# Expert selection in front of the one-hot table, an earlier pump, and w1's first remainders on VectorE

## The chip, the cores and the metric

The kernel runs on one core of one Trainium2 chip. The engines are TensorE (PE in the profile; its weight loads are PEld), VectorE (DVE), ScalarE (ACT), GpSimd (POOL) and SyncE (SP), and 16 DMA engines. The metric is the device time of one execution in microseconds (us).

## The reference

Three stages follow one another: windowed attention, a mixture of experts with one expert per token, and a dense feed-forward layer with a squared ReLU.

```python
# q, k, v: (4, 8, 576, 64); heads 0-3: 32 keys back; heads 4-7: 128 keys back, every 4th
scores = np.where(masks, q @ k.T / 8, -1e9)
x = softmax(scores) @ v              # -> (2304, 512)
logits = x @ w_gate + modality_bias[modality_id]
e_idx = np.argmax(logits, axis=1)    # one of 8 experts per token
for e in range(8):
    mask = e_idx == e
    h = np.maximum(x[mask] @ w1[e], 0.0)        # w1: (512, 1024) per expert
    out[mask] = gate_w[mask, None] * (h @ w2[e])  # w2: (1024, 512) per expert
h = np.maximum(out @ w_in, 0.0)      # w_in: (512, 2048)
result = h * h @ w_out
```

With the inputs of this case all tokens go to two experts.

## The kernel before, in words

Attention is cut into 48 units: 4 batches, two kinds of mask, 6 tiles of 96 queries. `schedule` runs rounds i = 0, 1, 2, ...; one round does the scores of unit i (`A`, lines 323 and 326), the transposes of x for the gate of unit i - 5 (`H`, L401), the transposes of the probabilities of unit i - 2 (`D`, L348), the product with v of unit i - 3 (`F`, L362, with the three VectorE instructions L365, L368 and L371) and, at the end of each group of six, the gate's logits. Every engine executes its instructions in the order in which this loop issues them.

Between these pieces `schedule` lets two other streams advance. `filler` runs matmuls of the experts' slots: it is called twice a round with FILL / 2 each, and each step of the stream costs an amount that is drawn from it. `step` runs the routing of a finished batch: `route` turns the logits of 576 tokens into positions (small VectorE instructions, L442 to L514), builds one-hots (L520, L521; on GpSimd, for batch 2 on VectorE), waits LATE[b] rounds, and multiplies the one-hots on TensorE (L527) into the table `tbl` of token numbers by expert column (L528 to L532). `select` (from L534) then chooses for two or four slots of 128 tokens which expert and which column of the table they take, some twenty VectorE instructions on one partition, and ends by casting the table to `itab` (L634).

When a batch's `side` stream is over, `schedule` calls `moe.pump`. It begins up to three slots (`begin`: SP and GpSimd load numbers from `esel`; GpSimd copies a column of itab to sc, L706, and gathers 128 rows of x from DRAM, L707, 128x513 words, 262 KB) and then stages weights (`stage`, L677: SP issues the DMAs of 2 MB each for w1 and w2 of slot 0). SP also stores x (L375, L379), and loads q, k and v (L298, L306, L294); GpSimd also scales q (L304).

A slot's work is: transposes of the gathered rows (`tx`, L714), xh on ScalarE and xl on VectorE; splitting w1 into a rounded part (ScalarE, L686) and a remainder (L687); the first layer (L728); transposes of its result (`th`, L741) with hth on ScalarE and htl on VectorE (L744); the second layer (L758). Slot 0 waits six empty filler calls between the pump and its transposes. Both weights are split for slot 0; later slots split only where the expert changes. In the function `split`, the first two remainders of w1 of slot 0 go to GpSimd, all others to VectorE.

After the attention the remaining slots run together with the decoding of w_in and w_out, and then the feed-forward layer, which is the longest part.

Of the kernel before, what the change touches and what calls it, by code (L numbers as in the profile page):

```python
# [11 lines left out]
F32 = mybir.dt.float32  # L12
F32R = mybir.dt.float32r
BF16 = mybir.dt.bfloat16
F16 = mybir.dt.float16
# [3 lines left out]
ALU = mybir.AluOpType  # L19
# [9 lines left out]
QT, KT = 96, 128  # L29
# [5 lines left out]
NCOL = E * NTT  # L35
TPB = S // QT
# [2 lines left out]
NA = 6  # L39
UPB = 2 * TPB  # L40
WAVES = ((0, 2), (2, 4), (NA, NSLOT - NA))
RATE, RATE1, RATE2, FILL, BURST, GAP = 0.35, 0.5, 0.5, 3.0, 0.0, 3
SETUP = 3
START = (("q", 0, 3), ("m", 0, 0), ("i", 0, 0), ("v", 0, 3), ("q", 3, 6), ("v", 3, 6))
LATE = (5, 5, 2, 7)
TINY = float(np.array([0x38100000], np.int32).view(np.float32)[0])


# [16 lines left out]
def body(ctx, tc, ins, out):  # L65
# [15 lines left out]
    with ExitStack() as mctx:  # L81
        moe = Moe(g, mctx)
        with ExitStack() as actx:
            att = Attention(g, actx)
            att.warm(9)
            with tc.manual_schedule():
                schedule(att, moe)
        ffn = Ffn(g, ctx)
        with tc.manual_schedule():
            for cost in moe.slots(NA, NTT):  # L90
                if not cost:
                    ffn.side()
            ffn.rest()
            moe.extras()
            moe.tag()
            ffn.l1(0, 0)
            ffn.l1(0, 1)
            run(moe.l2(NSLOT - 1))
        mctx.close()
        ffn.run()  # L100
# [6 lines left out]
def run(steps):  # L107
    for _ in steps:
        pass


def schedule(att, moe):
    nu = B * UPB
    moe.banks((2, 4), (4, 2), (2, 2), (7, 7))
    side, fc, sc, hold, nxt, due = None, 0.0, 0.0, 0, 0, 0
    i = 0
    fill, more = moe.slots(0, NA), True

    def step(cost):
        nonlocal side, sc, hold  # L120
        if i < hold:
            return
        sc += cost
        while side is not None and sc > 0 and i >= hold:
            c = next(side, None)
            if c is None:
                side = None
            elif c == 0:
                hold, sc = i + 1, 0.0
            else:  # L130
                sc -= c
        sc = min(sc, 0.0)

    def one():
        step(0.01 - sc)

    def filler(cost, late):
        nonlocal more, fc
        fc += cost
        while more and fc > 0:  # L140
            c = next(fill, None)
            if c is None:
                more = False
            elif c == -2 and late:
                fc = max(fc, BURST)
            elif c < 0:
                fc = 0.0
            else:
                fc -= c
        fc = min(fc, 0.0)  # L150

    for i in itertools.count():
        att.tail = i >= nu + 2
        ns, no, nh = (2, (5,), (5,)) if att.tail else (2, (5,), (6,)) if moe.ready else (3, (5, 4), (7,))
        r = RATE2 if i >= nu + 5 else RATE1 if moe.prepped else RATE
        if i == nu + 2:
            moe.banks((2, 4), (6, 0), (1, 1), (7, 3))
        att.A(i, (0, 1, 2)[:ns])
        if i == SETUP:
            att.setup()  # L160
        if NTL < i <= nu + 5 and i % NTL == 5:
            att.logits(i // NTL - 1, 1)
            if moe.ready and not att.tail:
                no, nh = nh, no
        if i > hold:
            step(r)
        att.H(i - 5, nh)
        filler(FILL / 2, False)
        att.D(i - 2)
        step(r)  # L170
        att.F(i - 3, no, one)
        att.C(i)
        filler(FILL / 2, True)
        step(r)
        if NTL < i <= nu + 5 and i % NTL == 4:
            att.logits(i // NTL - 1, 0)
        if due and side is None:
            moe.ready = sum(WAVES[due - 1])
            moe.pump()
            due = 0  # L180
        if nxt < B and side is None and i >= (nxt + 1) * UPB + 5:
            side = itertools.chain(att.route(nxt), att.select(*WAVES[nxt - 1]) if nxt else ())
            due, sc, hold = nxt, 0.0, i + 1
            nxt += 1
        if not more:
            break
    run(side or ())
    if due:
        moe.ready = NSLOT
        moe.pump()  # L190


class Attention:
# [236 lines left out]
    def route(self, b):  # L430
        nc, rt, iota = self.g.nc, self.rt, self.g.iota

        def new(shape, name, dt=F32):
            return rt.tile(shape, dt, tag=name, name=name)
# [3 lines left out]
        for i in range(TPB):  # L438
# [17 lines left out]
                                       op0=ALU.is_equal, op1=ALU.mult)  # L456
# [53 lines left out]
        cf, rf = new([QT, TPB], "rcf"), new([QT, TPB], "rrf")  # L510
# [1 line left out]
        nc.vector.tensor_copy(cf, ci)  # L512
        yield 0.12
        nc.vector.tensor_copy(rf, ri)  # L514
        rhot, val = new([QT, TPB, 128], "rhot", F16), new([QT, TPB, NCOL], "rval", F16)
        eng = nc.vector if b == 2 else nc.gpsimd
        for i in range(TPB):
            if b == 2:
                yield 0.5
            eng.tensor_scalar(out=rhot[:, i, :], in0=iota[:QT, :128], scalar1=rf[:, i:i + 1], scalar2=None, op0=ALU.is_equal)  # L520
            eng.tensor_scalar(out=val[:, i, :], in0=iota[:QT, :], scalar1=cf[:, i:i + 1],  # L521
                              scalar2=self.tok[:, i:i + 1], op0=ALU.is_equal, op1=ALU.mult)
        for _ in range(LATE[b]):
            yield 0
        psi = self.bank()[:, :NCOL]
# [1 line left out]
            nc.tensor.matmul(psi, rhot[:, i, :], val[:, i, :], start=i == 0, stop=i == TPB - 1)  # L527
        nc.vector.tensor_tensor(out=self.tbl, in0=psi, in1=self.tbl, op=ALU.add)  # L528
        if b:
            off = new([128, NCOL], "roff")  # L530
            nc.vector.tensor_scalar(out=off, in0=psi, scalar1=float(b * S), scalar2=float(b * S), op0=ALU.mult, op1=ALU.min)
            nc.vector.tensor_tensor(out=self.tbl, in0=self.tbl, in1=off, op=ALU.add)  # L532

    def select(self, j0, n):  # L534
        nc, rt, g = self.g.nc, self.rt, self.g
        last = j0 + n == NSLOT
        k = f"{j0}"

        def new(shape, name, dt=F32):
            return rt.tile(shape, dt, tag=name, name=name)  # L540
# [21 lines left out]
                                in1=cum.unsqueeze(1).to_broadcast([1, n, E]), op=ALU.is_ge)  # L562
# [27 lines left out]
        w = new([1, NSLOT, E], "sw")[:, :n, :]  # L590
# [38 lines left out]
            yield 0.12  # L629
            nc.vector.tensor_tensor(out=self.taken, in0=self.taken, in1=tk, op=ALU.add)  # L630

        it = g.moe.itab[{0: 0, 2: 1, 6: 2}[j0]]
        yield 0.12
        nc.vector.tensor_scalar(out=it, in0=self.tbl, scalar1=-1.0, scalar2=0.0, op0=ALU.add, op1=ALU.max)  # L634
        for j in range(j0, j0 + n):
            g.moe.itab_of[j] = it


class Moe:
    def __init__(self, g, ctx):  # L640
# [38 lines left out]
    def split(self, j, w):  # L679
        nc, tc = self.g.nc, self.g.tc  # L680
        c = self.chg[j][2]
        src, hi, lo = self.st[w], self.wh[w], self.wl[w]
        n = src.shape[1]

        def part(k, eng=nc.vector):
            nc.scalar.activation(out=hi[:, k, :], in_=src[:, k, :], func=AF.Copy)  # L686
            eng.tensor_tensor(out=lo[:, k, :], in0=src[:, k, :], in1=hi[:, k, :].bitcast(F32), op=ALU.subtract)  # L687

        if j == 0:
            for k in range(n):  # L690
                part(k, nc.gpsimd if w == 0 and k < 2 else nc.vector)
                yield -1
            return
        with tc.If(c > 0, preferred_fallthrough_block=False):
            for k in range(n):
                part(k)

    def begin(self, j):
        nc, g = self.g.nc, self.g
        e = nc.values_load(g.esel[0:1, 0, j:j + 1], engines=(ET.SP,), min_val=0, max_val=E - 1)  # L700
        c = nc.values_load(g.esel[0:1, 1, j:j + 1], engines=(ET.SP,), min_val=0, max_val=1)
        split = nc.values_load(g.esel[0:1, 1, j:j + 1], engines=(ET.Activation, ET.DVE), min_val=0, max_val=1)
        col = nc.values_load(g.esel[0:1, 2, j:j + 1], engines=(ET.Pool,), min_val=0, max_val=NCOL - 1)
        self.chg[j] = (e, c, split)
        sc = self.sc[j % 3]
        nc.gpsimd.tensor_copy(sc, self.itab_of[j][:, bass.ds(col, 1)])  # L706
        nc.gpsimd.indirect_dma_start(out=self.gx[j % 3], out_offset=None, in_=g.xd[0:2 * S if j < 2 else 3 * S if j < 6 else NT, :],  # L707
                                     in_offset=bass.IndirectOffsetOnAxis(ap=sc.bitcast(U32), axis=0))
# [375 lines left out]
```

## Time and profile before

| | us |
|---|---|
| median of 3 runs | 816.04 |
| lowest and highest | 813.96, 816.46 |
| the profiled execution | 815.87 |
| its span | 814.1 |
| TensorE busy | 784.6 (96%) |
| VectorE busy | 418.9 (51%) |
| ScalarE busy | 325.1 (40%) |
| GpSimd busy | 173.9 (21%) |

The mean granted TensorE clock was 0.99 of full speed. Times of the profile count from the start of the span. A row of a timeline has the start, the time to the end of the group, the engine, the line, the operation, output and inputs, and in square brackets how long the engine had been idle before it and what ended that; "x4" means four instructions in one row. "Busy" of a matmul group overlaps its neighbours a little, so the distance of two starts is the better measure of what a group takes. In a table of windows each row is a stretch with its length, then the busy time and the number of instructions of PE, PEld, DVE, ACT and POOL in this order, the granted clock (1.00 is full speed), the DMA engines' busy share and GB/s.

### The profile page before, as it was taken

The numbers are of one execution on the slowest core, as the hardware profiler recorded it, in microseconds if no ns is written. First come the engines' busy times: TensorE is split into PE (matmuls) and PEld (weight loads), VectorE is DVE, ScalarE is ACT, GpSimd is POOL, SyncE is SP. The second block draws the span as 40 slices with busy tenths as digits, with TensorE's granted clock in tenths as the row PEclk, the third lists the DMA queues.
The fourth block names the chain that finished last, engine by engine and source line by source line (L and its number), as shares of the span: only waits on it lengthen the run. The fifth ranks groups of instructions, "written<-read, shape, count | busy, mean of one in ns | idle before, by whom it ended". The sixth has DMA issues, their size and how long they took to land.

```text
span 814.1 us, 12599 instructions
## 1 busy us (share of the span) xinstructions
PE 784.6 (96%) x4273; PEld 671.7 (83%) x4273; DVE 418.9 (51%) x1124; ACT 325.1 (40%) x779; POOL 173.9 (21%) x234
## 2 busy tenths in 40 slices
PE   8999987899999999998989899999999999999996
PEld 5888866788888888887877799989989989998995
DVE  5787888444257777441799942242242233224222
ACT  5777766232245554541444522232232222223221
POOL 4254731231123333110255610010000001001001
PEclk9999998999999999999999999999999999999999
DMA  7766681201234443722245410010001001001001
GB/s 225 188 177 163 177 279 43 68 27 46 72 118 119 140 130 100 247 91 72 80 115 147 127 39 26 1 52 27 1 13 39 27 14 39 1 0 39 1 1 39
DMA packets 44810, 67.40 MB, mean 83 GB/s; under 512 B 6816, under 2 KB 28672, under 8 KB 44224
## 3 DMA queue, kind: packets, MB, share of 16 engines
q1 hardware_dynamic: 38720, 50.75, 21.6%
q0 software_dynamic: 3280, 10.76, 4.3%
q10 hardware_dynamic: 2736, 4.99, 1.6%
q8 instruction: 35, 0.57, 0.3%
q14 instruction: 39, 0.32, 0.1%
HBM read 129.65 MB, written 14.44 MB: 177 GB/s over the span
## 4 chain that ended last, share of the span: by engine, by line
issue 40%; DVE 5%; PE 2%; DMA 2%; POOL 1%; ACT 1%; POOLq 0%; ACTq 0%; DVEq 0%; SPq 0%
DMA raw<-in_wo 2%; POOL out L995 1%; DVE da L880 1%; PE bk L945 1%; DVE fhl L964 1%; DVE da L874 1%; DVE da L869 1%; PE bk L758 1%; DVE da L877 1%; PE bk L990 1%; ACT dm L867 0%; ACT woh L884 0%; DVE fsq L955 0%; DVE yl L932 0%; DVE fout L994 0%
## 5 line engine op out<-in xcount | busy, mean ns | idle before, releaser
L955 DVE TENSOR_TENSOR fsq<-fr 128x384 f32<-128x384 f32 x84 | 46.9, 559 | 173.3 <-ACT fr L953 173.3
L945 PE MATMUL bk<-yh,wih 128*128 128x384 f32 x384 | 130.7, 340 | 3.2 <-ACTq L827 1.6
L945 PE MATMUL bk<-yl,wih 128*128 128x384 f32 x384 | 130.3, 339 | 1.3 <-DVE yl L932 1.3
L945 PE MATMUL bk<-yh,wil 128*128 128x384 f32 x384 | 129.9, 338 | 0.0
L953 ACT ACTIVATE fr<-bk 128x384 f32<-128x384 f32 x96 | 46.9, 488 | 187.9 <-PE bk L945 187.3
L990 PE MATMUL bk<-woh,fhh 128*128 128x512 f32 x288 | 114.6, 398 | 2.7 <-ACT woh L884 2.7
L990 PE MATMUL bk<-wol,fhh 128*128 128x512 f32 x288 | 113.4, 394 | 2.9 <-POOL wol L885 2.9
L990 PE MATMUL bk<-woh,fhl 128*128 128x512 f32 x288 | 113.3, 393 | 0.0
L995 POOL DMA_INDIRECT out<-fout,fidx x18 | 18.1, 1006 | 323.3 <-DVE fout L994 320.5
L945 PEld LDWEIGHTS bk<-yh,wih 128*128 128x128 f32 x384 | 72.6, 189 | 8.3 <-ACT yh L931 2.2
L964 DVE TENSOR_TENSOR fhl<-fsq,fhh 128x384 fp32r<-128x384 f32 x96 | 55.4, 578 | 45.0 <-ACT fhh L963 44.7
L945 PEld LDWEIGHTS bk<-yl,wih 128*128 128x128 f32 x384 | 72.7, 189 | 5.8 <-DVE yl L932 2.6
L945 PEld LDWEIGHTS bk<-yh,wil 128*128 128x128 f32 x384 | 72.7, 189 | 0.0
L963 ACT ACTIVATE fhh<-fsq 128x384 fp32r<-128x384 f32 x96 | 50.4, 525 | 50.2 <-DVE fsq L955 48.7
L990 PEld LDWEIGHTS bk<-wol,fhh 128*128 128x128 f32 x288 | 54.1, 188 | 14.2 <-POOL wol L885 5.9
L728 PE MATMUL bk<-w1h,xh 128*128 128x512 f32 x152 | 64.1, 421 | 0.8 <-DVE htl L744 0.8
L990 PEld LDWEIGHTS bk<-woh,fhl 128*128 128x128 f32 x288 | 54.0, 188 | 12.9 <-DVE fhl L964 0.4
L990 PEld LDWEIGHTS bk<-woh,fhh 128*128 128x128 f32 x288 | 54.1, 188 | 12.2 <-ACT woh L884 4.2
L728 PE MATMUL bk<-w1l,xh 128*128 128x512 f32 x152 | 61.6, 405 | 0.0
L728 PE MATMUL bk<-w1h,xl 128*128 128x512 f32 x152 | 61.5, 404 | 0.0
L758 PE MATMUL bk<-w2h,hth 128*128 128x512 f32 x152 | 61.0, 401 | 0.0
L758 PE MATMUL bk<-w2h,htl 128*128 128x512 f32 x152 | 59.5, 391 | 0.0
(173 smaller groups left out, 1375.9 us busy)
## 6 DMA issues: line engine op xcount, KB each, us to landing
st<-in_w SPq DMA_DIRECT2D x41, 2048.0 KB
raw<-in_wi SPq DMA_DIRECT2D x32, 256.0 KB
raw<-in_wo SPq DMA_DIRECT2D x32, 256.0 KB
v<-in_v SPq DMA_DIRECT2D x7, 780.0 KB
q<-in_q SPq DMA_DIRECT2D x7, 576.0 KB
kd<-in_k SPq DMA_DIRECT2D x14, 288.0 KB
xd<-x SPq DMA_DIRECT2D x40, 96.0 KB
yb<-y ACTq DMA_DIRECT2D x13, 256.5 KB
```

Source lines behind the costliest of these rows:

```text
L728: nc.tensor.matmul(ps, a[:, c, :], w[:, c, sl], start=k == 0, stop=k == 11)
L758: nc.tensor.matmul(ps, a[:, c, :], w[:, c, :], start=k == 0, stop=k == 23)
L869: nc.vector.tensor_scalar(out=a, in0=raws[new][:, :, 1], scalar1=3, scalar2=0x3FFFFFF8, op0=ALU.logical_shift_left, op1=ALU.bitwise_and)
L874: nc.vector.scalar_tensor_tensor(out=a, in0=raws.pop(old)[:, :, 0], scalar=29, in1=a, op0=ALU.logical_shift_right, op1=ALU.bitwise_or)
L877: nc.vector.scalar_tensor_tensor(out=a, in0=raws[new][:, :, 1], scalar=-0x40000000, in1=a, op0=ALU.bitwise_and, op1=ALU.bitwise_or)
L945: nc.tensor.matmul(ps, w[:, c, f * 128:(f + 1) * 128], a[:, c, :], start=k == 0, stop=k == 11)
L953: nc.scalar.activation(out=r, in_=ps, func=AF.Relu)
L955: (nc.gpsimd if blk == 0 and f > 3 else nc.vector).tensor_tensor(out=s, in0=r, in1=r, op=ALU.mult)
L963: nc.scalar.activation(out=hh, in_=s, func=AF.Copy)
L964: nc.vector.tensor_tensor(out=hl, in0=s, in1=hh.bitcast(F32), op=ALU.subtract)
L990: nc.tensor.matmul(acc[t], a[:, sl], w[:, f, :], start=f == 0 and j == 0, stop=f == NF - 1 and j == 2)
L995: dma = nc.gpsimd.indirect_dma_start(out=out, out_offset=bass.IndirectOffsetOnAxis(ap=self.idx[:, i:i + 1].bitcast(U32), axis=0), in_=o, i ...
```

## The change

The one-hots move into a function `onehots`, the table into `table`, and a new generator `batch` runs `route`, then `select`, then `table`. Before, the order was route with the table, then select. For batches 0, 1 and 3 the one-hots are still issued at the end of `route`, on GpSimd; for batch 2 they are issued in `table`, on VectorE. `itab` is now made at the end of `table`. The rounds between the one-hots and their matmuls, LATE, go from 5, 5, 2, 7 to 5, 2, 1, 4. FILL goes from 3.0 to 2.0. In `split` the first two remainders of w1 go to VectorE with the others.

```diff
-RATE, RATE1, RATE2, FILL, BURST, GAP = 0.35, 0.5, 0.5, 3.0, 0.0, 3
+RATE, RATE1, RATE2, FILL, BURST, GAP = 0.35, 0.5, 0.5, 2.0, 0.0, 3
-LATE = (5, 5, 2, 7)
+LATE = (5, 2, 1, 4)
@@ schedule
-            side = itertools.chain(att.route(nxt), att.select(*WAVES[nxt - 1]) if nxt else ())
+            side = att.batch(nxt)
@@ route
-        rhot, val = new([QT, TPB, 128], "rhot", F16), new([QT, TPB, NCOL], "rval", F16)
+        self.hots = cf, rf, new([QT, TPB, 128], "rhot", F16), new([QT, TPB, NCOL], "rval", F16)
+        if b != 2:
+            yield from self.onehots(b)
+
+    def onehots(self, b):
+        nc, iota = self.g.nc, self.g.iota
+        cf, rf, rhot, val = self.hots
         eng = nc.vector if b == 2 else nc.gpsimd
         for i in range(TPB):
-            if b == 2:
-                yield 0.5
+            yield 0.5 if b == 2 else 0.01
             eng.tensor_scalar(out=rhot[:, i, :], ...)
             eng.tensor_scalar(out=val[:, i, :], ...)
+
+    def table(self, b):
+        nc, rt = self.g.nc, self.rt
+        rhot, val = self.hots[2:]
+        if b == 2:
+            yield from self.onehots(b)
         for _ in range(LATE[b]):
             yield 0
         psi = self.bank()[:, :NCOL]
...
             nc.vector.tensor_tensor(out=self.tbl, in0=self.tbl, in1=off, op=ALU.add)
+            yield 0.12
+            it = self.g.moe.itab[b - 1]
+            nc.vector.tensor_scalar(out=it, in0=self.tbl, scalar1=-1.0, scalar2=0.0, op0=ALU.add, op1=ALU.max)
+
+    def batch(self, b):
+        moe = self.g.moe
+        yield from self.route(b)
+        if b:
+            j0, n = WAVES[b - 1]
+            yield from self.select(j0, n)
+            for j in range(j0, j0 + n):
+                moe.itab_of[j] = moe.itab[b - 1]
+        yield from self.table(b)
@@ select
-        it = g.moe.itab[{0: 0, 2: 1, 6: 2}[j0]]
-        yield 0.12
-        nc.vector.tensor_scalar(out=it, in0=self.tbl, scalar1=-1.0, scalar2=0.0, op0=ALU.add, op1=ALU.max)
-        for j in range(j0, j0 + n):
-            g.moe.itab_of[j] = it
@@ split
-        def part(k, eng=nc.vector):
+        def part(k):
             nc.scalar.activation(out=hi[:, k, :], in_=src[:, k, :], func=AF.Copy)
-            eng.tensor_tensor(out=lo[:, k, :], in0=src[:, k, :], in1=hi[:, k, :].bitcast(F32), op=ALU.subtract)
+            nc.vector.tensor_tensor(out=lo[:, k, :], in0=src[:, k, :], in1=hi[:, k, :].bitcast(F32), op=ALU.subtract)
         if j == 0:
             for k in range(n):
-                part(k, nc.gpsimd if w == 0 and k < 2 else nc.vector)
+                part(k)
                 yield -1
```

The lines of the kernel after are some 18 higher in the experts' part: L714 becomes L732, L728 becomes L746, L707 becomes L725 and L677 becomes L695; the table's matmuls L527 become L538.

SP's queue around the first weights (st_81 is w1, st_82 is w2, xd<-x a store of x, esel the numbers of the chosen experts), in the kernel before:

```order
L379 DMA xd<-x 96x256
L379 DMA xd<-x 48x256 x2
L379 DMA xd<-x 96x256
L294 DMA v<-in_v 128x1560
L375 DMA xd<-x 96x256 x2
L700 TENSOR_LOAD esel
...
L677 DMA st_81<-in_w 128x4096
...
L677 DMA st_82<-in_w 128x4096
```

and in the kernel after:

```order
L379 DMA xd<-x 48x256 x2
L718 TENSOR_LOAD esel
...
L695 DMA st_81<-in_w 128x4096
...
L695 DMA st_82<-in_w 128x4096
L379 DMA xd<-x 96x256
L294 DMA v<-in_v 128x1560
L375 DMA xd<-x 96x256 x4
```

The weights have moved ahead of one load of v and three stores of x.

GpSimd's queue around the first gather, in the kernel after (q scaling, the load of the column number, the copy of the column, the gather):

```order
L526 TENSOR_SCALAR rval<-iota,rcf,tok 96x144
L304 TENSOR_SCALAR q<-q 128x192 [waits DMAHW0_49,PE_49,Pool_49]
L304 TENSOR_SCALAR q<-q 128x192 x5
L721 TENSOR_LOAD esel [waits DVE_49]
...
L724 COPY sc_97<-itab_104 128x1 [waits DVE_49]
L725 DMA gx_90<-xd,sc_97 128x513 [waits DMAHW5_49,DMAHW6_49,DMAHW3_49,DMAHW7_49,DMAHW2_49,Pool_49]
```

Here nothing has moved: before, too, the first gather stands right behind the same six scalings of q.

TensorE's queue in round 41 (L422 are the logits, L401 the transposes of x, L348 those of the probabilities), in the kernel before:

```order
L326 MATMUL bk_67<-kd_139,q 96x256 x2
...
L401 MATMUL bk_71<-ident,x 128x96 x2
L348 MATMUL bk_69<-ident,p 128x96 x4
L362 MATMUL bk_72<-v,pt 96x65 x4
L323 LDWEIGHTS mask
```

and in the kernel after:

```order
L422 MATMUL bk_72<-xtl,wg 16x288
L401 MATMUL bk_71<-ident,x 128x96 x2
L732 MATMUL bk_68<-ident,gx_90 128x128 x4
L348 MATMUL bk_69<-ident,p 128x96 x4
L362 MATMUL bk_72<-v,pt 96x65 x4
```

Slot 0's transposes now stand in round 41; before they stand at the same place of round 44.

## Rows read from the trace of the kernel before

**Rows 1.** Busy time of each engine, whole span (page, first part).
```profile
PE 784.6 (96%) x4273; PEld 671.7 (83%) x4273; DVE 418.9 (51%) x1124; ACT 325.1 (40%) x779; POOL 173.9 (21%) x234
```

**Rows 2.** Windows: stretch, length, PE, PEld, DVE, ACT, POOL busy, clock, DMA, GB/s.
```profile
94.58:96.81 2.23, 2.23 (x21) 1.94 (x21) 1.70 (x5) 1.83 (x7) 2.23 (x4) 1.00 0.62 96
106.90:146.45 39.55, 31.93 (x223) 25.57 (x222) 33.62 (x105) 25.62 (x67) 7.02 (x5) 0.91 0.42 144
110.90:121.70 10.80, 9.43 (x80) 8.07 (x81) 9.47 (x44) 8.13 (x24) 1.36 (x1) 1.00 0.94 364
126.20:133.00 6.80, 6.20 (x21) 4.85 (x22) 6.73 (x17) 2.68 (x7) 0.00 (x0) 0.50 0.07 19
146.60:150.10 3.50, 3.50 (x9) 2.73 (x10) 2.59 (x22) 0.00 (x0) 0.18 (x1) 0.51 0.05 15
```

**Rows 3.** Timeline of TensorE, 96 to 152 us.
```profile
97.89 0.33 PE L401 MATMUL bk<-ident,x 96*128 96x96 f32 x2
98.06 0.49 PE L348 MATMUL bk<-ident,p 96*128 96x96 f32 x4
98.39 0.54 PE L527 MATMUL bk<-rval,rhot 96*128 96x144 f16 x6
98.77 0.84 PE L362 MATMUL bk<-v,pt 128*96 128x65 f32 x8
...
107.53 0.33 PE L401 MATMUL bk<-ident,x 96*128 96x96 f32 x2
...
116.68 0.60 PE L714 MATMUL bk<-ident,gx 128*128 128x128 f32 x4
...
126.81 1.54 PE L362 MATMUL bk<-v,pt 128*96 128x65 f32 x8 [3.04 <-DVE x L371]
...
146.49 0.68 PE L728 MATMUL bk<-w1h,xh 128*128 128x512 f32 x1 [0.76 <-DVE htl L744]
```

**Rows 4.** Timeline of GpSimd, 99 to 130 us.
```profile
99.66 4.01 POOL L304 TENSOR_SCALAR q<-q 128x192 f32<-128x192 f32 x6 [2.74 <-PE bk L362]
...
107.44 1.18 POOL L707 DMA_INDIRECT gx<-xd,sc  x1 [0.85 <-DMA v<-in_v]
...
109.10 0.98 POOL L707 DMA_INDIRECT gx<-xd,sc  x1 [0.27 <-POOL sc L706]
120.34 4.67 POOL L687 TENSOR_TENSOR w1l<-st,w1h 128x1024 fp32r<-128x1024 f32 x2 [10.27 <-ACT w1h L686]
```

**Rows 5.** Timeline of VectorE, 99 to 144 us.
```profile
99.75 0.30 DVE L544 TENSOR_SCALAR sci<-carry 1x8 int32<-1x8 f32 x1
...
105.65 0.21 DVE L634 TENSOR_SCALAR itab<-tbl 128x144 int32<-128x144 f32 x1
...
120.93 1.80 DVE L514 CAST rrf<-rri 96x6 f32<-96x6 int32 x1
...
122.92 2.18 DVE L520 TENSOR_SCALAR rhot<-iota,rrf 96x128 f16<-96x128 f32 x1
...
125.36 0.27 DVE L520 TENSOR_SCALAR rhot<-iota,rrf 96x128 f16<-96x128 f32 x1
...
126.68 1.21 DVE L687 TENSOR_TENSOR w1l<-st,w1h 128x1024 fp32r<-128x1024 f32 x1
...
143.32 0.15 DVE L544 TENSOR_SCALAR sci<-carry 1x8 int32<-1x8 f32 x1
```

**Rows 6.** Timeline of SP's DMA issues, 98 to 99 and 106 to 110 us.
```profile
97.86 0.78 SPq L379 DMA_DIRECT2D xd<-x  x2
...
106.43 0.30 SPq L375 DMA_DIRECT2D xd<-x  x1
109.58 0.38 SPq L677 DMA_DIRECT2D st<-in_w  x1
```

**Rows 7.** Gathers by tile gx, 104 to 120 us: two gathers.
```profile
DMA to landing us min/median/max: 3.5/6.2/8.8
```

**Rows 8.** Gathers by tile gx, 320 to 336 us: two gathers.
```profile
DMA to landing us min/median/max: 3.8/6.9/10.0
```

More of the change, by code (lines that the diff above doesn't have):

```diff
@@ L529, in route @@
         if b:
-            off = new([128, NCOL], "roff")
+            off = rt.tile([128, NCOL], F32, tag="roff", name="roff")
             nc.vector.tensor_scalar(out=off, in0=psi, scalar1=float(b * S), scalar2=float(b * S), op0=ALU.mult, op1=ALU.min)
             nc.vector.tensor_tensor(out=self.tbl, in0=self.tbl, in1=off, op=ALU.add)
+            yield 0.12
[10 more added lines that the diff above has]
+        yield from self.table(b)
     def select(self, j0, n):
```

## The prediction

> **What bounds the kernel now.** I read the page first: TensorE (PE) is busy 784.6 of 814.1 us [rows 1]. So an edit pays only where PE waits, and I looked at PE's idle time by windows. Outside the decode of wi and wo, which the change does not touch, PE waits in one stretch: 106.9 to 146.45, between the selection for batch 1 and the start of slot 1's first matmuls. There PE is busy 31.93 of 39.55 us, the mean granted clock is 0.91, and VectorE (DVE) is busy 33.62 [rows 2]. VectorE has more to do there than in a plain round of attention, where it is busy 1.70 of 2.23 us [rows 2]: the splits of both weights, xl, htl, the routing of batch 2 and its one-hots. PE follows it.
>
> The timeline of PE gives the marks [rows 3]: in round 41 it starts the x transposes (L401) at 107.53; slot 0's transposes (L714) stand three rounds later, at 116.68; the longest wait, 3.04 us, ends at 126.81; and slot 1's first matmul starts at 146.49, when htl's second half is in. This last one is my milestone: behind it VectorE has slack and PE stays nearly full in both kernels, so a gain or loss there goes straight to the end. Around the 3.04 us of waiting the granted clock fell to 0.50, the lower of the two levels, and stayed there from 126.2 to 133.0; it cost little, since VectorE was busy 6.73 of these 6.80 us [rows 2]. It was 0.51 again from 146.6 to 150.1, behind the milestone, where PE was busy all the time [rows 2]: half of 3.5 us, 1.7, is lost there.
>
> What made the 3.04 us is in VectorE's and GpSimd's (POOL's) timelines side by side. GpSimd ran the first two remainders of w1, 4.67 us from 120.34 [rows 4]. In that time a small cast at VectorE's L514 took 1.80, and the one-hot L520 took 2.18, against 0.27 for the same L520 at 125.36 [rows 5]. With 0.16 for the small cast (the price of the small copies beside it, an estimate) the two lost 3.55 us.
>
> **The change, part by part.**
>
> *Remainders on VectorE.* Two of 1.21 [rows 5] are added, 2.42 less an overlap with the neighbours of 0.15, 2.27; 3.55 go. Net gain 1.3 on the engine that bounds the stretch. GpSimd's 4.67 fall away where nothing waited for it.
>
> *Selection ahead of the table, table two rounds after the one-hots.* Batch 1's selection moves from rounds 38 to 40 to rounds 33 to 35, where VectorE has 0.5 us a round free [rows 2], beside GpSimd's one-hots. The only rows with selection beside GpSimd are those at 99.75: L544 0.30 against 0.15 at 143.32 [rows 5], while GpSimd scaled q [rows 4]. Twenty operations at +0.15 are 3.0 us over three rounds, against 1.6 free; so up to 1.4 late, down to nothing if most overlap. But rounds 38 to 40 get the room back that the selection took there until 105.65 [rows 5]. I take zero, with 0.6 either way. The Trainium skill, "SBUF — State Buffer", section "SBUF: two separate sides", says that GpSimd and a VectorE instruction with two SBUF inputs share a port pair as an exclusive lock, the other blocks for the whole instruction. By that rule the 2.18 is the wait for one remainder of 2.36, and the trace agrees there; the selection beside q scaling it overstates, for no row there waits out a whole scaling of 0.68.
>
> *The pump three rounds earlier.* Selection and itab end in round 37, so SP issues the weights and GpSimd the gathers about 7 us sooner, and slot 0's transposes stand in round 41, right behind the L401 that began at 107.53. The two issuers don't move alike, and this is the term that decides.
>
> SP: in the order after, the esel loads follow the two half x stores of round 37, which SP issued by 98.64 [rows 6]. From the last x store's end (106.73) to the first weight DMA (109.58) the loads took 2.85; so the weights are issued at about 101.5 and 102.1 and, as before (when 121.7 was the end, 12.1 us behind the issue; 364 GB/s on the mean from 110.9 on [rows 2]), are in by about 113.6. The v load that stood ahead of them now stands behind both; it lands about 115.5, and round 45 needs it, later than that: no cost.
>
> POOL: the six q scalings still stand ahead of the first esel load. They started at 99.66, when q had come, and ended at 103.67 [rows 4]; q's load and the rounds around it don't move. Before, 1.6 us passed from itab's end (105.65 + 0.21) to the gather at 107.44 [rows 4, 5], with the load of the column number partly ahead of it; I take 2, an estimate, so gather 0 is issued at about 105.7, four microseconds behind the weights. Before, gather 0 was issued at 107.44, ahead of them, and landed in 3.5; gather 1, issued at 109.10 with the weights right behind it, took 8.8 [rows 4, 7]. In a later slot a gather beside weights took 10.0, the other 3.8 [rows 8]. A gather behind the weights thus lands with their end. I take 8.8: 114.5; bounds 109.2 (3.5) and 115.7 (10.0).
>
> PE reaches slot 0's transposes at about 107.2 (a little sooner than 107.53, since rounds 38 to 40 carry no selection), executes in order, and waits until 114.5: 7.3 us idle, VectorE soon too. Queued behind are the whole of round 41's rest and all that follows.
>
> *The sum to the milestone.* VectorE's own work before, 106.9 to 146.45: 33.62 − 3.55 = 30.1. After, to the same htl: + 2.27; + 16 selection operations of batch 2, which now precede it, at 0.15 less overlaps, 1.9; − the table's three, 0.8, − one pair of one-hots, 0.5, − two attention tails (x and two small ones), 1.1, − one remainder of the transposed x, 0.3: 31.7, an estimate. Some 1.8 of it, about what a round has, lies ahead of the wait. After the landing: 0.6 for four transposes and 0.65 for xh, so xl starts at 115.75; 29.9 of VectorE work; gaps, of which the stretch had 5.9 before, 3 to 4: the milestone at about 149.1. Up to there PE has done less than before: two groups each of L401, L348, L362 and the six table matmuls. By the starts from 97.89 to 98.77 and L362's 0.84, less some 0.18 by which it overlaps what follows [rows 3], that is 2 × (0.17 + 0.33 + 0.66) + 0.38 = 2.7. So 149.1 + 2.7 = 151.8 stands against 146.49 + 1.7 = 148.2: +3.6.
>
> *Slot 2's transposes.* They stand some 4 us of PE work behind batch 2's table matmuls, before 13. Table to itab is four operations, 1.2; itab to gather issue was 1.8 (105.65 to 107.44) and the landing 3.5 [rows 4, 5, 7]: 6.5 against 4 to 5.5. I take +1, from 0 to 2.5.
>
> *Batch 3's table, the smaller FILL.* One slot sooner, its gather beside no weights; PE work is the same and VectorE has slack: nothing, unless a copy waits (0.3). The smaller share moves matmuls of the slots into later rounds and beyond the attention, where they fill PE as well; its part at the milestone is in the counts above.
>
> Sum: the profiled execution took 815.87 with a span of 814.1, 0.17 under the median. +3.6 + 1 gives 820.5; I say 820, since work that piles up in the wait may fill VectorE's gaps better. If the clock falls again behind the milestone, 1.7 is to be added: 822. That is some 4 above the median; a difference under 0.3%, 2.45 us, I call none.
>
> **Rivals.**
>
> *A. The gather is hardly delayed; VectorE's gaps stay.* Landing at 109.5 to 111, PE waits 2 to 4. xl starts at 110.8 to 112.3, the milestone is 144 to 146, and the total 816 ± 1.5. For it: a gather is 262 KB, the weights 4.2 MB. Against it: the two rows of 8.8 and 10.0. The Trainium skill, "DMA: Bandwidth & Descriptors", section "Queues, rings and completion order", says that each DMA engine takes turns between queues packet by packet. That would double some 0.7 us of transfer (262 KB at 364 GB/s, an estimate) and speaks for A; the 8.8 and 10.0 are against it.
>
> *B. Faster: the early weights feed VectorE without gaps.* As in A the gather comes by 110; and both weights being in when w1's splits begin, VectorE, without port stalls, works through its 29.9 with 0 to 1 us of gaps: milestone 141, + 2.7 = 143.7, less 148.2: −4.5, so about 811.5. It decides if the gather lands before about 111. For it: before, PE's 3.04 and its half clock came out of the port stall that goes. Against it: gaps are also handovers from PE and ScalarE, which stay.
>
> *C. Slower by another place.* The gather is in time but selection beside the one-hots stalls VectorE (1.4 in rounds 33 to 36), the table waits for the one-hots (0.5) and slot 2's transposes wait 2.5: +4.4 against a gain of about 1.2 at the milestone: 819. It decides if the stalls reach 1 us and slot 2's gather lands 6 us behind the table.
>
> **How the numbers follow.** The late gather 0.48 (its own range 817 to 824: landing at 112 with nothing at slot 2, to landing at 115.7 with 2.5 there), C 0.07, A 0.24, B 0.21. Time 820. The range: from B's end, 811.8, to the worst late case, 824. Faster by over 0.3%: B and the lower edge of A, 0.24. Within: A's rest and the soft edge of the late gather, 0.26. Slower: 0.50.
>
> **What would show it.** Right: gather 0's DMA issued about 105.7 and landing after 113; the first weights issued at 101.5; PE idle 6 to 8 us just ahead of slot 0's transposes, and the clock at 0.5 behind that wait; L514 and L520 back at 0.15 and 0.27; slot 1's first matmul at 148 to 150; a short wait ahead of slot 2's transposes. Wrong: the gather landing by 110, or q scaled before 99, or PE's idle time moved to another place. If the forecast time comes with the gather early, the mechanism is C's.

## The result, and the profile after

The changed kernel takes 825.04 us (median of 4 runs, 823.82 to 825.92), the kernel before 815.68 (4 runs): slower, ratio 1.0116 with a 95% interval of 1.0096 to 1.0136. The forecast was 820, from 811.8 to 824: the direction was right, the size was not, and 825.04 lies above the range. The profiled execution took 824.48, 8.6 more than the one of before.

The first part of the page, first line, and four windows of the kernel after (columns as in [rows 2]):

```profile
PE 783.2 (95%) x4273; PEld 670.3 (81%) x4273; DVE 418.1 (51%) x1126; ACT 325.9 (40%) x779; POOL 170.3 (21%) x232
```

```profile
106.90:152.18 45.28, 31.41 (x194) 25.04 (x192) 31.58 (x113) 25.03 (x65) 1.41 (x3) 0.85 0.34 132
115.20:118.00 2.80, 2.75 (x16) 2.75 (x17) 0.81 (x3) 1.55 (x5) 0.00 (x0) 0.50 0.96 390
118.00:128.10 10.10, 5.57 (x38) 4.27 (x38) 7.86 (x21) 7.03 (x17) 0.00 (x0) 0.84 0.30 108
128.20:133.00 4.80, 4.80 (x18) 3.93 (x18) 4.31 (x17) 1.92 (x6) 0.00 (x0) 0.50 0.13 21
```

TensorE ran the same 4273 matmuls and its busy time is the same to a microsecond and a half (784.6 in [rows 1]), so what grew is its idle time. To the milestone, slot 1's first matmul, VectorE was busy 31.58 us; the prediction had counted 31.7. But the stretch lasts 45.28 where it lasted 39.55 [rows 2].

The timelines of GpSimd, SP and TensorE show why:

```profile
101.57 3.97 POOL L304 TENSOR_SCALAR q<-q 128x192 f32<-128x192 f32 x6 [3.06 <-DMA q<-in_q]
105.49 0.18 POOL L724 COPY sc<-itab 128x1 int32 x1
105.97 1.18 POOL L725 DMA_INDIRECT gx<-xd,sc  x1 [0.30 <-POOL sc L724]
```

```profile
104.40 0.94 SPq L695 DMA_DIRECT2D st<-in_w  x2
105.44 0.37 SPq L379 DMA_DIRECT2D xd<-x  x1
105.90 0.63 SPq L294 DMA_DIRECT2D v<-in_v  x1
```

```profile
108.48 0.33 PE L401 MATMUL bk<-ident,x 96*128 96x96 f32 x2
115.25 1.12 PE L732 MATMUL bk<-ident,gx 128*128 128x128 f32 x4 [6.44 <-DMA gx<-xd,sc]
...
128.18 0.20 PE L465 MATMUL bk<-roh,ones 96*96 96x48 f16 x1 [3.66 <-DVE xtl L405]
...
152.18 0.50 PE L746 MATMUL bk<-w1h,xh 128*128 128x512 f32 x1 [1.93 <-DVE htl L762]
...
161.80 0.66 PE L732 MATMUL bk<-ident,gx 128*128 128x128 f32 x4 [0.34 <-DMA gx<-xd,sc]
```

The gather stands behind the six q scalings, is issued 1.6 us behind the weights, and TensorE waits 6.44 us for it. The wait shown in [rows 3] at L362, 3.04, is gone. In its place stand 3.66 at L465 and 1.93 at the milestone. Behind the waits of 6.44 and 3.66 the granted clock was 0.50, the lower level (the windows from 115.20 and from 128.20); by the 0.84 of the window between them, the first fall lasted some 3 us beyond 118.00 (an estimate).

VectorE, answering to [rows 5], with the two kinds of GpSimd work beside the selection ahead of it:

```profile
85.96 4.01 POOL L304 TENSOR_SCALAR q<-q 128x192 f32<-128x192 f32 x6 [11.22 <-PE bk L362]
89.96 0.61 POOL L525 TENSOR_SCALAR rhot<-iota,rrf 96x128 f16<-96x128 f32 x1
```

```profile
88.38 0.30 DVE L568 TENSOR_SCALAR sci<-carry 1x8 int32<-1x8 f32 x1
...
90.56 0.15 DVE L591 TENSOR_TENSOR ssel<-sge 1x12 f32<-1x12 f32 x1
...
126.04 1.23 DVE L705 TENSOR_TENSOR w1l<-st,w1h 128x1024 fp32r<-128x1024 f32 x1 [1.22 <-ACT w1h L704]
...
137.75 0.17 DVE L514 CAST rrf<-rri 96x6 f32<-96x6 int32 x1
137.83 0.15 DVE L568 TENSOR_SCALAR sci<-carry 1x8 int32<-1x8 f32 x1
...
146.48 0.27 DVE L525 TENSOR_SCALAR rhot<-iota,rrf 96x128 f16<-96x128 f32 x1
```

Batch 2's cast at L514 took 0.17 (it was 1.80), and its first one-hot, which now stands behind the splits, 0.27 (it was 2.18); GpSimd had nothing to run beside either. Batch 1's selection began beside q scaling once more, and its first instruction took 0.30 there and 0.15 alone, the same pair as in [rows 5]. Most of it ran beside the one-hots, from 89.96 on. There L591 took 0.15; its counterpart in the kernel before took twice that beside q scaling:

```profile
102.35 0.33 DVE L567 TENSOR_TENSOR ssel<-sge 1x12 f32<-1x12 f32 x1
```

Of the fifteen selection instructions from 90.04 to 94.00, apart from a memset, twelve took 0.13 to 0.16 and three 0.22 to 0.28.

### The profile page after: what moved, and what is told of

Its sections match the earlier page's. It is cut to its first block, busy times and chain, and to the rows that moved or that the text cites. A ratio compares the mean times of both kernels' runs of the same rounds, so it can differ in the third digit from the quotient of the medians.

```text
span 822.7 us, 12596 instructions
## 1 busy us (share of the span) xinstructions
PE 783.2 (95%) x4273; PEld 670.3 (81%) x4273; DVE 418.1 (51%) x1126; ACT 325.9 (40%) x779; POOL 170.3 (21%) x232
## 4 chain that ended last, share of the span: by engine, by line
issue 40%; DVE 6%; DMA 2%; POOL 2%; PE 1%; ACT 1%; POOLq 0%; ACTq 0%; DVEq 0%; SPq 0%
DMA raw<-in_wo 2%; DVE da L898 2%; POOL out L1013 1%; DVE da L892 1%; DVE fhl L982 1%; DVE da L887 1%; PE bk L776 1%; DVE da L895 1%; PE bk L963 1%; ACT dm L885 0%; DVE fsq L973 0%; ACT woh L902 0%; PE bk L1008 0%; DVE fout L1012 0%; ACT fhh L981 0%
## 5 line engine op out<-in xcount | busy, mean ns | idle before, releaser
L746 PE MATMUL bk<-w1h,xh 128*128 128x512 f32 x152 | 63.3, 417 | 1.9 <-DVE htl L762 1.9
L746 PE MATMUL bk<-w1h,xl 128*128 128x512 f32 x152 | 60.7, 399 | 0.0
L746 PE MATMUL bk<-w1l,xh 128*128 128x512 f32 x152 | 60.7, 399 | 0.0
```

The lines of the kernel that those rows point to most:

```text
L746: nc.tensor.matmul(ps, a[:, c, :], w[:, c, sl], start=k == 0, stop=k == 11)
```

## The experiments

Ratios are to the kernel before on the same chip, with 95% intervals. "After" in a title means that the edit is made to the changed kernel.

**After, q scaled behind the gathers.**

```diff
-                for t in range(t0, t1):
-                    q = self.qt[g][:, t]
-                    nc.gpsimd.tensor_scalar(out=q, in0=q, scalar1=0.125, ...)
+                self.unscaled = (g, t0, t1)   # scale() issues the same six instructions
+                if g != 7:
+                    self.scale()
@@ schedule
             moe.pump()
+            att.scale()
```

> The kernel after, with the six q scalings of the last group (L304) issued on GpSimd behind the first two gathers instead of ahead of them; nothing else moves. Theory G (the gather lands with the end of the weights, TensorE waits 6.4 us for it): gather 0 is issued about 101, some 3 us ahead of the weights, lands by 106, the wait ahead of slot 0's transposes is under 0.5 us, the clock stays at 1.00 there, and the time is 816 to 818.5. Theory V (VectorE's work bounds the stretch and the wait only moves to it): the wait at the transposes goes, waits for VectorE grow by the same, 822 to 825.

Measured 819.05, ratio 1.0038 (1.0016 to 1.0059); after stood at 1.0116. GpSimd, TensorE and ScalarE of this kernel (its lines are 9 higher):

```profile
100.82 1.19 POOL L734 DMA_INDIRECT gx<-xd,sc  x1 [0.86 <-DMA q<-in_q]
```

```profile
108.29 0.60 PE L741 MATMUL bk<-ident,gx 128*128 128x128 f32 x4
...
115.23 0.66 PE L448 MATMUL bk<-ident,lt 16*96 16x16 f32 x6 [3.36 <-DVE xtl L414]
```

```profile
112.00 1.06 ACT L713 ACTIVATE w1h<-st 128x1024 fp32r<-128x1024 f32 x1 [1.09 <-DMA st<-in_w]
```

```profile
115.23:121.00 5.77, 5.22 (x25) 4.23 (x26) 4.44 (x13) 3.35 (x8) 0.00 (x0) 0.50 0.72 260
```

Theory G holds for the wait: the gather is issued at 100.8, ahead of the weights, TensorE doesn't wait for it, and some 6 us come back. But 3.4 us of waiting now stand seven microseconds later, behind a split that began only when w1 was in at 112.00; behind that wait the clock fell to 0.50 (the window), and the kernel is still slower than before. Neither theory had the size: the wait for the gather is not the whole loss.

**After, weights two rounds later.** `moe.pump()` begins the slots without staging; a second `moe.pump()` two rounds later stages.

```diff
-            moe.pump()
+            moe.pump(due > 1)
+            late = i + 2 if due == 1 else 0
             due = 0
+        elif late and i == late:
+            moe.pump()
```

> The kernel after, with SP issuing slot 0's two weight DMAs two rounds later than the gathers (end of round 39 instead of 37). Theory G: weights issued about 109, gather 0 issued at 106 lands at 109.5 to 110, TensorE waits about 1 us for it, time 816.5 to 819. Theory V: the early weights are what keeps VectorE fed; without them w1's splits come later, 822 to 826.

Measured 827.1, ratio 1.0128 (1.0085 to 1.0171). This run doesn't separate the theories: q came later in it (its scaling began at 104.88), so the gather was issued at 109.28, again behind the weights (108.06), and TensorE waited 6.91 for it. It is one more sample of a gather behind weights.

**After, FILL 3.0.** One number: `FILL = 3.0`.

> The kernel after with FILL back at 3.0. Theory G: the wait for the gather is the same 6.4 us, time 824 to 826; the smaller share is worth under 1 us either way. Theory F (the smaller share leaves TensorE without matmuls while VectorE works): the waits behind the transposes shrink by 3 to 5 us, 819 to 822.

Measured 828.71, ratio 1.0160 (1.0114 to 1.0206): a miss on both sides. 3.0 is the worse, though its interval overlaps that of after a little (1.0096 to 1.0136). The wait for the gather is there (5.6). The new loss is late; the longest idle times of TensorE from 150 to 172, and a window of the same kernel:

```profile
164.50 0.96 PE L362 MATMUL bk<-v,pt 128*96 128x65 f32 x8 [1.80 <-DVE xtl L405]
166.38 0.58 PE L401 MATMUL bk<-ident,x 96*128 96x96 f32 x2 [0.91 <-DVE x L371]
167.77 0.58 PE L401 MATMUL bk<-ident,x 96*128 96x96 f32 x2 [0.81 <-DVE xtl L405]
169.16 0.42 PE L422 MATMUL bk<-xth,wg 128*16 128x288 f32 x1 [0.81 <-DVE xtl L405]
```

```profile
164.50:174.00 9.50, 5.69 (x25) 3.33 (x25) 3.48 (x10) 1.26 (x3) 0.00 (x0) 0.54 0.09 28
```

What slots 0 and 1 had to give was used up before batch 2's pump, so slot 2 too had to wait GAP rounds of empty filler calls; its transposes came only at 171.78, and the last rounds of attention ran bare: TensorE 5.69 of 9.50 busy, at a clock of 0.54.

**After, two remainders on GpSimd.** `part(k, nc.gpsimd if w == 0 and k < 2 else nc.vector)` again.

> The kernel after with the first two remainders of w1 back on GpSimd. Theory G: it makes no difference to the wait for the gather; VectorE saves 2.4 us of its own work and loses 2 to 3.5 behind the shared port, so 824 to 827. Theory R (the remainders on VectorE are what makes the new 3.66 us wait at L465): that wait falls under 1 us and the time is 821 to 823.

Measured 826.19, ratio 1.0115 (1.0071 to 1.0159): no difference from after that this run can tell. The wait at L465 was 4.5, so theory R falls.

**After, GAP 6.** `GAP = 6`, where GAP is the number of rounds with empty filler calls between the pump and the transposes: slot 0's transposes are back in round 44.

> The kernel after with GAP 6 instead of 3, so that slot 0's transposes stand in round 44 again (as before) while the pump, the gathers and the weights stay three rounds earlier. Theory G (the wait for the gather): TensorE reaches the transposes at about 115.5, the gather is in at 115, wait under 0.5, time 815 to 818. Theory L (what costs is the later, thinner stretch itself: smaller FILL, table of batch 2 late): 822 to 825.

Measured 820.8, ratio 1.0062 (1.0037 to 1.0087). The transposes stood at 117.91 without a wait, some 4 us came back, and 5 stayed, which is between the two theories. So with the late transposes something else of the change still costs; FILL was the part not yet tried there.

**After, q scaled behind the gathers, GAP 4.** `GAP = 4` on top of the first experiment.

> The kernel with the q scalings behind the gathers (819.05), and GAP 4, which puts slot 0's transposes one round later, into round 42. Theory W (there the wait only moved on to the weights: ScalarE's first w1h waited until w1 was in at 112.0, VectorE's remainder stood behind it, TensorE waited 3.36 us at the logits' transposes L448): with 2.2 us more the weights are in, that wait falls to about 1 us, time 816.5 to 818. Theory N (VectorE's load alone makes these waits): 818.5 to 820.5.

Measured 821.07, ratio 1.0063 (1.0031 to 1.0095). The 3.36 at the logits' transposes went, and 3.8 came twice at the routing's matmuls (L474), at 120.03 for batch 2 and at 169.29 for batch 3. Theory W is not supported: later transposes didn't help here.

**Before, the remainders alone.** In the kernel before, `part(k)` for all.

> The kernel before with only one edit: the first two remainders of w1 on VectorE. By the prediction's term VectorE saves 3.55 of blocking and pays 2.27: 814 to 815.5. Rival: VectorE's queue then stands behind ScalarE's w1h too, which the remainders on GpSimd did not make it do: 816 to 818.

Measured 814.66, ratio 0.9985 (0.9967 to 1.0003). L514 took 0.15 again, and the wait of 3.04 became 2.26. The sign is as the prediction's term had it, with a size that reaches to nothing.

**Before, FILL 2.0 alone.** One number in the kernel before.

> The kernel before with only FILL at 2.0. If a smaller share is good by itself (in the kernel after 3.0 cost 3.7 us), 812 to 814.5; if it is good only where the table of batch 2 comes late, because the filler does not run dry, 815 to 817.

Measured 819.11, ratio 1.0039 (1.0022 to 1.0056): both expectations missed; the smaller share alone costs 3.6. One window from the end of [rows 3]'s longest wait to the last rounds of attention, of the kernel before and of this one:

```profile
126.80:160.40 33.60, 31.28 (x169) 25.20 (x170) 21.57 (x76) 14.34 (x35) 4.66 (x8) 0.86 0.18 50
```

```profile
126.80:160.40 33.60, 27.68 (x152) 21.63 (x153) 21.50 (x76) 13.95 (x34) 3.49 (x6) 0.85 0.16 42
```

VectorE does the same (21.57 and 21.50), TensorE 3.6 us less beside it; 0.4 of that is the end of the same wait, which is over at 127.22 here. The new waits of TensorE in this window are these:

```profile
145.93 0.39 PE L401 MATMUL bk<-ident,x 96*128 96x96 f32 x2 [1.67 <-DVEq L694]
...
148.66 1.54 PE L362 MATMUL bk<-v,pt 128*96 128x65 f32 x8 [1.90 <-DVE xtl L405]
```

So I read the mechanism: while a round waits for VectorE, the slots' matmuls are TensorE's cover, and a smaller share of them per round leaves it idle there. The matmuls come later, in time that was full before. VectorE itself is not full in this window (21.5 of 33.6): what a round waits for is the chain through it and ScalarE, not its load alone.

**After, GAP 6 and FILL 3.0.** Both numbers: TensorE's matmuls stand as before, but for batch 1's table.

> The kernel after with GAP 6 and FILL 3.0: TensorE's matmuls stand in the order of the kernel before, but for batch 1's table, one round earlier; selection first, early gathers and weights, and the remainders on VectorE stay. Theory S (what costs is where the slots' matmuls stand: slot 0's transposes ahead of the gather's landing, and the share of filler; selection beside the one-hots costs about 1, the remainders give about 1): 814.5 to 817. Theory C (something else of the early pump costs, the v load behind the weights for one, 1.4 us of waiting in round 44 of the kernel with GAP 6 and FILL 2.0): 818 to 821.

Measured 815.27, ratio 0.9992 (0.9978 to 1.0006): the whole loss is gone, with selection first, early weights and gathers and the remainders all still there. TensorE of this kernel:

```profile
118.15 0.60 PE L732 MATMUL bk<-ident,gx 128*128 128x128 f32 x4
...
140.02 0.38 PE L401 MATMUL bk<-ident,x 96*128 96x96 f32 x2 [2.08 <-DVE x L371]
...
147.02 0.50 PE L746 MATMUL bk<-w1h,xh 128*128 128x512 f32 x1 [0.42 <-issue]
```

This is what theory S had expected, and theory C falls: the v load behind the weights made one wait of 1.0 and no loss in the sum.

**After, w2's load later.** As the second experiment, with w1 staged at once and w2 three rounds later.

> The kernel after with only w2's load issued three rounds later than w1's (end of round 40). If a gather issued behind weights lands with the end of what is queued ahead of it, gather 0 now lands with w1, about 110.5 to 111.5 (issued 106, 5 us), TensorE's wait at slot 0's transposes falls from 6.4 to 2 to 3, and the time to 820.5 to 822.5. If a gather beside any weights takes 8.8 to 10 whatever their bytes: 114.5 again, 824 to 826; if engines took turns packet by packet, 4 to 4.5 us in both, which the kernel after has excluded already.

Measured 823.06, ratio 1.0101 (1.0062 to 1.0141). SP ran ahead and issued w2 at 107.31, only 3.2 behind w1; TensorE waited 4.89 instead of 6.44. Between the two expectations; the law of the gather's delay stays open.

**After, GAP 5 and FILL 3.0.** Transposes in round 43.

> The kernel after with GAP 5 and FILL 3.0: slot 0's transposes in round 43, one round earlier than in the kernel before; slot 1's matmuls end while batch 2's pump is done, so the filler does not run dry. By theory S the gather (landing about 115) is late by about 1 us at most and VectorE's load sets the stretch: 814.5 to 817.5. If starting the slots earlier than before is what loses, 818 to 821.

Measured 819.88, ratio 1.0054 (1.0032 to 1.0075). TensorE waited 2.1 for the gather, 1.9 for the logits' sum in the last rounds. Theory S had expected 814.5 to 817.5 and missed; the time lies in the rival's range, in which starting the slots earlier than before is itself what loses.

**TensorE's order as before, batch 2's one-hots on GpSimd.** Made from the experiments: FILL 3.0, GAP 3, batch 1's table ahead of its selection, remainders on VectorE. Against the kernel after:

```diff
@@ route
-        if b != 2:
-            yield from self.onehots(b)
+        yield from self.onehots(b)
@@ onehots and table: no case for b == 2
-        eng = nc.vector if b == 2 else nc.gpsimd
+        eng = nc.gpsimd
@@ batch
         yield from self.route(b)
+        if b == 1:
+            yield from self.table(b)
...
-        yield from self.table(b)
+        if b != 1:
+            yield from self.table(b)
```

with `LATE = (5, 5, 2, 4)` and `FILL = 3.0`.

> TensorE's order as in the kernel before (FILL 3.0, GAP 3, batch 1's table ahead of its selection), the remainders on VectorE, and batch 2's one-hots on GpSimd, with batch 2's selection ahead of its table. GpSimd is free of the remainders, so it has room for the one-hots. If VectorE's own work bounds 107 to 146 (theory S), 12 one-hot instructions, 2.8 us, leave it beside the 1.3 of the remainders: 811.5 to 813.5. If selection beside GpSimd's one-hots costs as it did for batch 1 (1.2), half of it goes: 813 to 814.5. If the waits are handovers and not load: 814.5 to 816.

Measured 813.27 (12 runs), ratio 0.9977 (0.9964 to 0.9991): faster than the kernel before by 0.2%, and than the one after. It is at the upper edge of what theory S had expected and also inside the second expectation, 813 to 814.5, so it does not tell the two apart. The longest wait of [rows 3] is 1.87 and the milestone stands at 145.09, 1.4 earlier:

```profile
125.61 1.54 PE L362 MATMUL bk<-v,pt 128*96 128x65 f32 x8 [1.87 <-DVE x L371]
...
145.09 0.51 PE L746 MATMUL bk<-w1h,xh 128*128 128x512 f32 x1 [0.75 <-DVE htl L762]
```

## Why the prediction was right in direction and wrong in size

The four kernels that differ only in two numbers, with all the rest of the change in them:

| | FILL 3.0 | FILL 2.0 |
|---|---|---|
| GAP 6 (transposes in round 44) | 0.9992 | 1.0062 |
| GAP 3 (transposes in round 41) | 1.0160 | 1.0116 (the change) |

*Remainders on VectorE*: the forecast was a gain of 1.3. Alone they gave 0.8 (interval from 2.7 gain to 0.2 loss); inside the change it can't be told. The stalls at L514 and L520 went as forecast.

*Selection ahead of the table*: taken as zero, with 0.6 either way and a bound of 1.4. The bound came from twenty operations at 0.15 more each beside GpSimd; beside the one-hots most took no longer than alone. Still, rounds 33 to 36 took 11.25 us (85.53 to 96.78) against 10.13 (84.45 to 94.58), 1.1 more. But the kernel with GAP 6 and FILL 3.0 has this loss too and is level with before, so the sum with the remainders and the rounds given back is about zero, as taken.

*The pump three rounds earlier*: the mechanism was right. The gather was issued at 105.97 (105.7 forecast), the transposes began at 115.25 (114.5 forecast), TensorE idled 6.44 (7.3). That the issue came within 0.3 of the forecast is luck: the q scalings, which were not to move, began 1.9 later (101.57 against 99.66), and from their end to the gather it took 0.4 and not the 2 that I had assumed. The weights went out at 104.40, not 101.5: SP's loads stood behind x stores that themselves came later. So the gather was 1.6 behind the weights and not four. Ordering the gathers first gave back 6.0 us, the largest term. Rival A would have had the gather in by 110; in the kernel after and in the two experiments on the weights' loads, each with the gather issued behind w1, TensorE stood until 115.25, 118.03 and 113.35. The Trainium skill, "DMA: Bandwidth & Descriptors", section "Queues, rings and completion order", says that each DMA engine takes turns between queues packet by packet. The trace disagrees with what I drew from it for A; why the gather is held longer than its share was not shown.

*The sum to the milestone*: here the prediction failed. The stretch from the start of xl to slot 1's first matmul, in the kernel before and in the kernel after:

```profile
118.07:146.49 28.42, 21.85 (x139) 17.21 (x137) 24.93 (x71) 18.89 (x46) 4.67 (x2) 0.88 0.28 89
```

```profile
117.04:152.18 35.14, 27.71 (x174) 22.04 (x173) 29.58 (x108) 23.78 (x61) 0.00 (x0) 0.86 0.16 52
```

VectorE's own work was right (29.58 against 29.9). The milestone stood at 152.18, not at 149.1; these 3.1 are the larger part of the 4.0 by which the profiled execution missed the sum of 820.5. Of them 1.3 were there when xl started, at 117.04 and not 115.75: the transposes began 0.75 later, and at the lower clock they took 1.12 and not 0.6. The prediction had named that fall of the clock and had given it no price. (Some of the 1.3 need not come of the change: the kernel after was 1.1 behind at round 30 already, 78.15 against 77.07, ahead of batch 1's selection.)

The step that failed is the term of the gaps, "3 to 4", and with it "*Batch 3's table, the smaller FILL* ... nothing". Behind the start of xl VectorE was idle for 5.6 of 35.14 (3.5 of 28.42 before). What the smaller share does to TensorE in this stretch is seen in the kernel after with FILL 3.0 and nothing else changed, in the same window as the first of the section on the result:

```profile
106.90:152.18 45.28, 35.41 (x212) 28.69 (x211) 32.38 (x118) 25.48 (x64) 1.23 (x3) 0.85 0.34 129
```

TensorE did 4.0 us more there than with FILL 2.0 (31.41), at the same mean clock and beside about the same work of VectorE; 0.8 of it is a shorter wait for the gather (5.60 against 6.44). I had argued that the smaller share only moves matmuls to where they fill TensorE as well. The single edit shows that this is not so in the kernel before, 3.6 us slower by itself, nor with the rest of the change at GAP 6, 5.7 slower (0.9992 to 1.0062). The cover that a matmul gives is worth something where TensorE would otherwise wait for the chain through VectorE; I took TensorE's work as conserved and did not ask at what time it is done. How much of VectorE's own 5.6 comes of the share, and how much of the longer stretch, was not shown. The remaining 0.9 of the miss lie behind the milestone and were not located.

*Why no single term adds up*: at GAP 3 the sign of FILL turns for the whole kernel (1.0160 to 1.0116): FILL 3.0 loses more behind this stretch than it gains in it. With early slots a large share uses up slots 0 and 1 before batch 2's pump, and the attention ends bare. So the change's FILL mends part of what its early transposes break, and FILL 3.0 would not have brought the change to its forecast. From before to after by one way: FILL alone +3.6, the rest +5.8. By another way, at FILL 2.0, the order of gather and q scaling alone is 6.0. TensorE's idle time and clock show the parts, in the kernel before, before with FILL 2.0, after, and after with FILL 3.0:

```profile
100.00:180.00 80.00, 70.88 (x432) 56.39 (x431) 54.57 (x211) 37.85 (x97) 20.41 (x28) 0.94 0.35 108
```

```profile
100.00:180.00 80.00, 68.27 (x420) 54.22 (x419) 53.12 (x209) 37.16 (x97) 24.32 (x32) 0.94 0.36 109
```

```profile
100.00:180.00 80.00, 64.66 (x408) 51.55 (x407) 50.93 (x192) 38.26 (x99) 11.41 (x19) 0.91 0.34 112
```

```profile
100.00:180.00 80.00, 64.46 (x386) 50.99 (x385) 46.32 (x163) 37.20 (x95) 11.07 (x18) 0.83 0.34 111
```

FILL 2.0 alone adds 2.6 of idle time at the same clock, so most of its 3.6 is idle time. The two kernels at GAP 3 are idle alike; what FILL 3.0 loses there against FILL 2.0 is the clock, 0.83 against 0.91.

*Slot 2's transposes*: the forecast was a wait of 1; it was 0.34, with a few waits under 0.6 around it.

*Rivals*: B (faster, VectorE without gaps) did not come true even with the gather early: 819.05 where it said 811.5. That experiment does not give B its whole condition, for w1 was in only at 112.00, after the transposes. What stood against B, handovers that stay, was there in the kernel after: VectorE's remainder waited 1.22 for ScalarE's half. C's stall was there, but not as the loss.

What stays open: how long a gather is held behind a given number of bytes, and why GAP 5 with FILL 3.0 loses 4.5 us where GAP 6 loses nothing; of its waits only the 2.1 for the gather is what theory S counts.

## What to carry to other kernels

Where one engine executes in order and another is late, the filler's worth depends on when it runs: price a smaller share in the stretch where the other engine holds it up, not over the whole. When a block is moved earlier, look at each queue by itself: here SP could move and GpSimd could not, and a short gather came behind four megabytes that it used to precede. And test knobs in pairs, since each of two numbers may look right only for the other's value.

## What was not expected of the hardware

In the fastest version GpSimd's one-hots ran beside VectorE's remainders. Some of their second instructions, which read three operands, took two to three times as long as the 0.85 of the last one shown, which had no remainder beside it (GpSimd's timeline of that kernel):

```profile
122.34 0.61 POOL L524 TENSOR_SCALAR rhot<-iota,rrf 96x128 f16<-96x128 f32 x1 [12.27 <-DVE sci L568]
122.96 1.89 POOL L525 TENSOR_SCALAR rval<-iota,rcf,tok 96x144 f16<-96x144 f32 x1
...
130.66 2.77 POOL L525 TENSOR_SCALAR rval<-iota,rcf,tok 96x144 f16<-96x144 f32 x1
...
134.00 0.85 POOL L525 TENSOR_SCALAR rval<-iota,rcf,tok 96x144 f16<-96x144 f32 x1
```

VectorE's remainders beside the two long ones:

```profile
122.91 1.20 DVE L705 TENSOR_TENSOR w1l<-st,w1h 128x1024 fp32r<-128x1024 f32 x1
...
130.90 1.88 DVE L705 TENSOR_TENSOR w2l<-st,w2h 128x512 fp32r<-128x512 f32 x3
```

GpSimd's instruction took longer than the 0.85 by 1.04 and 1.92, about what these remainders last, and they took no longer than elsewhere (1.23 and 1.21 in the kernels shown above). The GpSimd instruction at 130.66 had begun ahead of VectorE's run, and it was still the one that was held up. In the kernel before it was VectorE that stood, up to 2.18 for a 0.27 instruction [rows 5]; here it was GpSimd, whose work nobody waited for. Over the two kernels, then, the blocking went both ways, and the blocked engine that had slack is the one where it held up nobody.
